# A token transform of seven matmuls in place of nine, and a new order of the work around it

## The chip, the cores and the metric

The kernel runs on one core of a Trainium2 chip. The metric is the device time of one execution in microseconds. Five engines work side by side: TensorE (PE, with its weight loads as PEld), VectorE (DVE), ScalarE (ACT), GpSimd (POOL), and SyncE (SP), which issues most of the DMA transfers.

## The reference

There are two stages. The first, for 8 batches, 8 heads, 576 tokens and a head size of 64, is a linear attention with a norm; its outputs are put side by side as x of 8 x 576 x 512. The second adds a Fourier mix to x and runs a feed-forward layer with a residual:

```python
kv = np.einsum('bhsd,bhse->bhde', k, v)
out = np.einsum('bhsd,bhde->bhse', q, kv)
out = out / np.sqrt(np.mean(out * out, axis=-1, keepdims=True) + 1e-06) * g_norm
x = out.transpose(0, 2, 1, 3).reshape(B, S, H * D)
X = np.fft.fft(np.fft.fft(x, axis=1), axis=2)
u = x + np.real(X)
un = (u - mean(u)) / np.sqrt(var(u) + 1e-06)
out = u + np.maximum(un @ w_ch1, 0.0) @ w_ch2      # 512 -> 2048 -> 512
```

The FFT over axis 1 is the token transform, the FFT over axis 2 the channel transform.

## The kernel before

**Three passes for a product.** TensorE multiplies float32 numbers rounded to a shorter form (F32R). To keep the precision, an operand is split into a high part (rounded) and a low part (what the rounding left), and a product is three matmuls: high by high, high by low, low by high. The list `passes = [(0, 0), (0, 1), (1, 0)]` stands for that.

**Stages of a batch.** The functions `plan_kv`, `plan_q`, `plan_out` and `plan_y` load k, v and q and make x with its norm, in three tiles x of 96 token pairs each (a token and its mirror lie side by side in one row of 1024 columns; tile 0 has a 97th row, token 0). `plan_fold` scales a tile by the norm (DVE, L1097), folds the channels by their symmetry into `ab` (DVE, three instructions at L1109), makes sum and difference of the two halves into `xe` (POOL, L1119, two instructions), and splits that into `xh` (ACT, L1125) and `xl` (POOL, L1128). `plan_seq` is the token transform: for each of two parts (cosine, sine) and two channel halves, nine matmuls (three tiles by three passes) of 290 columns against the constants `cs`, 36 a batch (PE, L1146). Its results go through `far` (ACT) and `pt` (DVE) to `plan_chn`, the channel transform (PE, L1192), then `x` gets its mix (POOL, L1231 and L1234; DVE for the first batch), is stored, and is turned (`plan_turn`, PE, L1290) into `unTh` and `unTl`, columns of the input of the feed-forward layer.

**The feed-forward layer** works on 9 blocks of 512 tokens. For three of the sixteen slices of w1 and w2 a block is worked off as soon as it is turned (`plan_early`, L707 and L725, 72 matmuls a block); the rest of the layer follows after the batches (L1659, L1670, then L2021, L2056), from about 310 us to the end.

**The order of the work.** Everything up to there is given as operations with an engine, an estimated cost, a rank, what they come after and which buffers of which ring they hold. `Plan.run` plays them through with these costs: on each engine the ready operation of lowest rank whose buffers are free goes next, and the order so found is pinned instruction by instruction. The early feed-forward work has a high rank (`FILL`), so it fills what the batches leave on PE. Ranks are moved by the table `SHIFT`, one number for each stage, engine and rank. Rings bound how far ahead the work runs (`RINGS`: 9 tiles x, 4 tiles e2, 7 tiles for k and v, 3 pairs xh and xl). An operation marked `port`, and every POOL operation, are kept from running side by side in the plan.

**The spares.** `plan_spare` puts 92 matmuls without a use (L778) on PE: 30 at the start and 62 of the very last rank (`SPARE`), which the plan places where nothing else is ready. Their number is fixed.

**Single points.** `dft["s", part]` are the constants of the token transform: loaded into a tile of ring x (`draw`), split by ACT (L809) and POOL (L812). `x0` collects one sum for each token and batch (L1102); after the batches nine matmuls (`p0_mm`, L1485) transform it.

Of the kernel before, what the change touches and what calls it, by code (L numbers as in the profile page):

```python
# [9 lines left out]
F32 = mybir.dt.float32  # L10
F32R = mybir.dt.float32r
# [16 lines left out]
NA = 3  # L28
# [27 lines left out]
    ("", "DVE", -100): -1448,  # L56
    ("", "POOL", -40): 17.5,
    ("", "SP DMA", -40): -10141,
    ("", "HOST", 0): 1816.5,
    ("", "POOL", 10): -5.5,  # L60
    ("", "SP DMA", 10): -746.5,
    ("", "POOL", 20): 180,
    ("", "SP DMA", 20): 2640,
    ("", "POOL", 30): 416.5,
    ("", "POOL", 40): 214,
    ("", "POOL", 50): 610.5,
    ("", "POOL", 60): 997.5,
    ("", "POOL", 70): 1564.5,
    ("", "DVE", 85): 8704.5,
    ("", "PE", 85): 2564.5,  # L70
    ("", "SP DMA", 85): 250,
    ("", "HOST", 9000): 1111.5,
    ("chn", "ACT", -34): -184.5,
    ("chn", "DVE", -34): -1439,
    ("chn", "PE", -34): -83,
    ("chn", "SP DMA", -34): 402.5,
    ("chn", "DVE", 16): 595,
    ("chn", "PE", 16): -644,
    ("chn", "POOL", 16): 6,
# [12 lines left out]
    ("chn", "PE", 46): -80,
    ("chn", "POOL", 46): 1379.5,
    ("chn", "SP DMA", 46): -3012.5,
    ("chn", "ACT", 56): 1025,
    ("chn", "PE", 56): -25901.5,
    ("chn", "POOL", 56): -528.5,
    ("chn", "SP DMA", 56): -1527,
    ("chn", "ACT", 66): -31752.5,
    ("chn", "PE", 66): -52.5,  # L100
    ("chn", "POOL", 66): -3331,
    ("chn", "SP DMA", 66): 11254,
    ("chn", "DVE", 76): 25.5,
    ("chn", "PE", 76): -133,
    ("chn", "POOL", 76): -23.5,
    ("chn", "SP DMA", 76): -103.5,
    ("dft", "ACT", -37): 96.5,
    ("dft", "POOL", -37): -769.5,
    ("dft", "SP DMA", -37): -1260,
    ("dft_d", "ACT", -35): 29,  # L110
    ("dft_d", "DVE", -35): 260.5,
    ("dft_d", "POOL", -35): 759.5,
    ("dft_d", "SP DMA", -35): -1780,
    ("early", "ACT", -100): -3365,
    ("early", "DVE", -100): -6.5,
    ("early", "SP DMA", -100): -3677.5,
    ("early", "PE", 1010): 4339.5,
    ("early", "PE", 1020): 6953.5,
    ("early", "PE", 1030): -3681,
    ("early", "PE", 1040): -4341,  # L120
    ("early", "PE", 1050): 838.5,
    ("early", "PE", 1060): 298,
    ("early", "PE", 1070): -32396.5,
    ("early", "PE", 1080): -1466,
    ("fold", "ACT", -36): 250,
    ("fold", "DVE", -36): 678,
    ("fold", "ACT", 14): -1189.5,
    ("fold", "DVE", 14): -774,
    ("fold", "POOL", 14): 151.5,
    ("fold", "ACT", 24): 2956,  # L130
    ("fold", "DVE", 24): 4653,
    ("fold", "POOL", 24): 2218.5,
    ("fold", "ACT", 34): -660,
    ("fold", "DVE", 34): 389.5,
# [2114 lines left out]
```

## Time and profile before

| what | value |
|---|---|
| time, median of 3 runs | 966.81 us (966.07 to 968.41) |
| the profiled execution's own time | 966.81 us |
| its span, first to last instruction | 965.0 us |
| PE busy | 956.7 us (99%) |
| DVE, ACT, POOL busy | 683.8, 362.6, 438.3 us |
| granted TensorE clock | 1.000 over the whole span |
| DMA | 210 MB, mean 218 GB/s |

The busy time of an engine is the time in which at least one of its instructions is running; matmuls overlap, so the duration of one (390 ns for 512 columns) is longer than the distance from one to the next. "Idle before, releaser" says how long an engine had stood before an instruction, and which instruction or transfer it had waited for.

### The profile page before, as it was taken

The page shows a single profiled execution, that of the slowest core. Times are in us where ns is not written, and L with a number is a line of the kernel's source. Part 1 is how long each engine was busy: PE and PEld are TensorE (multiplying, and loading weights), DVE is VectorE, ACT ScalarE, POOL GpSimd, SP SyncE. Part 2 cuts the span into 40 slices and gives each one's busy share as a digit, 9 for nine tenths or more (in the row PEclk, how much of TensorE's full clock was granted, in tenths as well). Part 3 has the DMA queues.
Part 4 walks back from the last instruction along what each step waited for, and adds up shares of the span by engine and source line. Part 5 has one row for each costly group of instructions (what it writes and reads, how often), then busy time and mean ns, then how long its engine had stood idle before and what let it go on. Part 6 is the DMA issues. An engine that isn't in the chain of part 4 may idle for free.

```text
span 965.0 us, 15998 instructions
## 1 busy us (share of the span) xinstructions
PE 956.7 (99%) x5992; PEld 806.7 (84%) x5992; DVE 683.8 (71%) x1192; ACT 362.6 (38%) x685; POOL 438.3 (45%) x426
## 2 busy tenths in 40 slices
PE   9999999999999999999999999999999999999998
PEld 7888888988888888888888888888888888888886
DVE  4897867766868568999547967586757685674554
ACT  2655647575544323343313421342225222521110
POOL 2646767975854215666635043825472428210000
PEclk9999999999999999999999999999999999999999
DMA  9999979572475799987588496428642675213412
GB/s 239 211 258 273 253 217 277 130 229 88 158 289 192 283 325 309 367 305 275 220 307 329 162 362 246 187 87 292 240 165 93 231 275 209 88 66 126 189 68 87
DMA packets 112193, 210.00 MB, mean 218 GB/s; under 512 B 45150, under 2 KB 66226, under 8 KB 103156
## 3 DMA queue, kind: packets, MB, share of 16 engines
q1 hardware_dynamic: 109076, 199.54, 62.6%
q0 software_dynamic: 1920, 6.29, 1.8%
q10 hardware_dynamic: 1120, 3.15, 1.0%
q8 instruction: 47, 0.77, 0.3%
q14 instruction: 30, 0.25, 0.1%
HBM read 141.02 MB, written 67.93 MB: 217 GB/s over the span
## 4 chain that ended last, share of the span: by engine, by line
PE 97%; DVE 1%; DMA 1%; issue 0%; ACT 0%; POOL 0%; DVEq 0%; POOLq 0%; ACTq 0%
PE acc L2056 23%; PE ps_h L2021 20%; PE ps_h L1659 10%; PE acc L1670 10%; PE ps_h L707 8%; PE acc L725 8%; PE ps_f L1146 4%; PE ps_o L982 3%; PE ps_k L886 3%; PE ps_s L778 2%; PE ps_f L1192 2%; PE ps_q L955 2%; PE ps_t L1290 2%; DMA vm<-in_v_dram 1%; PE ps_w L666 1%
## 5 line engine op out<-in xcount | busy, mean ns | idle before, releaser
L2056 PE MATMUL acc<-w2c,hh 128*128 128x512 f32 x640 | 197.7, 390 | 0.0
L720 DVE SCALAR_TENSOR_TENSOR hl<-ps_h,hh 128x512 fp32r<-128x512 f32 x144 | 98.7, 688 | 109.2 <-ACT hh L717 102.7
L717 ACT ACTIVATE hh<-ps_h 128x512 fp32r<-128x512 f32 x144 | 85.8, 597 | 232.2 <-PE ps_h L2021 88.4
L2056 PEld LDWEIGHTS acc<-w2c,hh 128*128 128x128 f32 x640 | 119.7, 188 | 25.4
L2066 DVE TENSOR_TENSOR us<-acc,us 128x512 f32<-128x512 f32 (+1 forms) x161 | 106.9, 681 | 43.0 <-PE acc L2056 42.6
L2056 PE MATMUL acc<-w2c,hl 128*128 128x512 f32 x320 | 124.5, 389 | 0.0
L2021 PE MATMUL ps_h<-t,w1c 128*128 128x512 f32 x480 | 115.3, 389 | 0.0
L2021 PEld LDWEIGHTS ps_h<-t,w1c 128*128 128x128 f32 x480 | 90.1, 188 | 18.7
L2021 PE MATMUL ps_h<-b,w1c 128*128 128x512 f32 x360 | 91.2, 389 | 0.0
L1692 POOL TENSOR_TENSOR us<-us,low 128x512 f32<-128x512 f32 x30 | 45.5, 1521 | 99.8 <-ACT low L1689 93.8
L2021 PEld LDWEIGHTS ps_h<-b,w1c 128*128 128x128 f32 x360 | 67.6, 188 | 14.0
L2056 PEld LDWEIGHTS acc<-w2c,hl 128*128 128x128 f32 x320 | 60.1, 188 | 12.4
L725 PE MATMUL acc<-w,hh 128*128 128x512 f32 x216 | 67.9, 398 | 0.0
L707 PE MATMUL ps_h<-unTh,w 128*128 128x512 f32 x216 | 67.4, 393 | 0.0
L1670 PE MATMUL acc<-w,hh 128*128 128x512 f32 x216 | 64.6, 390 | 0.0
L1032 POOL TENSOR_TENSOR x<-x,gb 96x512 f32<-96x512 f32 (+1 forms) x36 | 46.4, 1305 | 30.2 <-ACT x L999 29.9
L1659 PE MATMUL ps_h<-unTh,w 128*128 128x512 f32 x192 | 59.9, 393 | 0.0
L1887 POOL TENSOR_TENSOR z<-z,low 128x512 f32<-128x512 f32 x24 | 31.0, 1296 | 58.1 <-DMA low<-unT_scr 56.7
L2038 DVE TENSOR_TENSOR ps_h<-ps_h,s 128x512 f32<-128x512 f32 x60 | 39.8, 693 | 13.8 <-PE ps_h L2021 13.2
L1670 PEld LDWEIGHTS acc<-w,hh 128*128 128x128 f32 x216 | 40.5, 188 | 8.4
L2123 ACT COPY s<-ps_h 128x512 f32<-128x512 f32 x20 | 11.7, 587 | 92.8 <-PE ps_h L2021 92.8
L707 PEld LDWEIGHTS ps_h<-unTh,w 128*128 128x128 f32 x216 | 39.9, 188 | 7.9
(183 smaller groups left out, 1984.7 us busy)
## 6 DMA issues: line engine op xcount, KB each, us to landing
w1c<-w_scr SPq DMA_DIRECT2D x13, 1792.0 KB
raw<-in_moe_w_ch_dram SPq DMA_DIRECT2D x32, 512.0 KB
w2c<-w_scr SPq DMA_DIRECT2D x14, 1024.0 KB
unT_scr<-unTh SPq DMA_DIRECT2D x9, 1024.0 KB
unT_scr<-unTl SPq DMA_DIRECT2D x9, 1024.0 KB
part_scr<-part SPq DMA_DIRECT2D x36, 256.0 KB
w_scr<-w1q SPq DMA_DIRECT2D x5, 1792.0 KB
km<-in_k_dram SPq DMA_DIRECT2D x29, 288.0 KB
```

Source lines behind the costliest of these rows:

```text
L707: nc.tensor.matmul(ps, w[c][:, kc * P : (kc + 1) * P], unT[a][:, kc, :], start=(idx == 0), stop=(idx == 3 * KC - 1),)
L717: nc.scalar.activation(hh, ps, AF.Relu)
L720: nc.vector.scalar_tensor_tensor(hl, ps, 0.0, hh.bitcast(F32), ALU.max, ALU.subtract)
L725: nc.tensor.matmul(acc, hpair[a][:, i * P : (i + 1) * P], w[c], start=(first and n == 0), stop=(last and n == 2),)
L1032: nc.gpsimd.tensor_tensor(v_, v_, gb[:n].unsqueeze(1).to_broadcast([n, H, D]), ALU.mult)
L1659: nc.tensor.matmul(ps, w1_of(f, c, kc), unTs[j][a][:, kc, :], start=(idx == 0), stop=(idx == 3 * KC - 1),)
L1670: nc.tensor.matmul(acc, hpair[a][:, i * P : (i + 1) * P], w2_of(f, c), start=(first_ and n == 0), stop=(last_ and n == 2),)
L1692: nc.gpsimd.tensor_tensor(ut, ut, part, ALU.add)
L2021: nc.tensor.matmul(ps, w[:, A_OF[m], c, kc * P : (kc + 1) * P], b[:, a, kc * BT : (kc + 1) * BT], start=(fresh and idx == 0), stop=(done a ...
L2038: nc.vector.tensor_tensor(to, a, b, ALU.add)
L2056: nc.tensor.matmul(ps, hpair[a][:, i * P : (i + 1) * P], w2c[n][:, r, c], start=(idx == 0), stop=(idx == 5),)
L2066: nc.vector.tensor_tensor(ut[:, cols], ps[:, cols], ut[:, cols], ALU.add)
```

## The change

From the second batch on, the third tile of 96 rows is taken apart into three groups of 32 rows. Two of them are put into the rows 96 to 127 of tiles 0 and 1, which so have 128 rows and take three matmuls each. The rest, 32 rows of tile 2 and two rows that both hold token 0, is put into a stacked tile `xst` of 98 rows in which the same 32 rows stand three times (twice rounded, once as the low part) against constants `css` laid out to match, so that one matmul does all three passes: 3 + 3 + 1 = 7. The first batch keeps nine, with the constants of its third tile in two tiles of ring x (`third`). The constants of the new rows are loaded and split once more (`plan_dft_rest`), after the matmuls of the first batch have read the rows that they overwrite. The sum and difference of the moved rows are made by DVE (`moved`, two instructions each, three times a batch) and the stacked tile by three ACT copies in place of one. The transform of `x0` has seven matmuls too, with more small DVE copies ahead of it. Ring e2 has 5 tiles for 4, the ring for k and v 6 for 7; tile 0 has 98 rows for 97 in every stage. All numbers of the table SHIFT are other ones, so the order on every engine is a new one up to about 310 us; the code of the rest is the same.

```diff
@@ the table of shifts @@
 SHIFT = {
-    ("", "DVE", -100): -1448,
-    ("", "POOL", -40): 17.5,
...
+    ("", "DVE", -100): -546.5,
...
 }
 RINGS = {
-    "p8": 8, "part": 2, "unT": 2, "h": 2 * NA, "qt": 2, "fq": 4, "kvt": 2, "kv": 7, "kr": 2, "x": 9, "raw": 2, "e2": 4, "wk": 2, "xhl": 3, "pt": 1, "two": 2, "far": 1,
+    "p8": 8, "part": 2, "unT": 2, "h": 2 * NA, "qt": 2, "fq": 4, "kvt": 2, "kv": 6, "kr": 2, "xst": 1, "x": 9, "raw": 2, "e2": 5, "wk": 2, "xhl": 3, "pt": 1, "two": 2, "far": 1,
 }
@@ sizes @@
-    rows = [TR + 1, TR, TR]
+    rows = [TR + 2, TR, TR]
+    Q4 = P - TR
+    KST = TR + 2
+    assert TR == 3 * Q4
     offs = [0, TR + 2, 2 * TR + 2]
@@ tiles @@
-    cs = cst.tile([TR + 1, 2, 2, 3, NS], F32R, name="cs")
+    cs = cst.tile([P, 2, 2, 2, NS], F32R, name="cs")
+    css = cst.tile([KST, 2, NS], F32R, name="css")
     cd = cst.tile([P, 2, 2, NE], F32, name="cd")

     paired = cst.tile([P, 1], F32, name="paired")
     nc.vector.tensor_scalar(paired, ident[:, P - 1 : P], -1.0, 1.0, ALU.mult, ALU.add)
-    x0 = cst.tile([TR + 1, 3, B], F32, name="x0")
+    x0 = cst.tile([P, 3, B], F32, name="x0")
...
@@ plan_dft @@
         raw = ring("x", one, [P, 2 * DM], "draw")
...
+        third[part] = ring("x", one, [P, 2 * DM], "third", F32R)
         flat = src[part].rearrange("p t c -> p (t c)")
...
+        dft["s", part] = plan_dft_split(
+            r, raw, ld, slice(0, n), slice(0, 2 * NS),
+            *[lambda c=c: dst[:n, part, c].rearrange("p t c -> p (t c)") for c in range(2)],
+        ) + plan_dft_split(
+            r, raw, ld, slice(0, TR), slice(2 * NS, 3 * NS),
+            *[lambda c=c: third[part].t[:TR, c * NS : (c + 1) * NS] for c in range(2)], [third[part]],
         )
-        dft[key, part] = c
+
+    def plan_dft_split(r, raw, ld, rows_, cols, hi, lo, bufs=()):
...
+        b = op(
+            "ACT", 100 + size, r,
+            lambda: nc.scalar.activation(hi(), raw.t[rows_, cols], AF.Copy), ld, [raw, *bufs],
+        )
+        if lo is None:
+            return [b]
+        return [op(
+            "POOL", 100 + 2.25 * size, r,
+            lambda: nc.gpsimd.tensor_tensor(lo(), raw.t[rows_, cols], hi().bitcast(F32), ALU.subtract),
+            [b], [raw, *bufs],
+        )]
+
+    def plan_dft_rest(part, used):
+        r = rank(1, SEQ) - 6
+        raw = ring("x", one, [P, 2 * DM], "drest")
+        s = dft_s[part]
+        own = slice(2 * NS, 3 * NS)
+        low_rows = slice(Q4, 2 * Q4)
+
+        def free():
+            return raw.t[TR:, : 2 * NS].rearrange("p (t c) -> p t c", t=2)
+
+        ld = [
+            dma(kb, r, lambda fn=fn: nc.sync.dma_start(*fn()), [], [raw])
+            for kb, fn in (
+                (80, lambda: (free(), s[: 2 * Q4, 2].rearrange("(t p) c -> p t c", t=2))),
+                *[(40, lambda g=g: (raw.t[g * Q4 : (g + 1) * Q4, own], s[2 * Q4 : TR, 2])) for g in range(3)],
+                (4, lambda: (raw.t[TR:KST, own], s[TR, 0].partition_broadcast(2))),
+            )
+        ]
+        done = plan_dft_split(
+            r, raw, ld[:1] + used, slice(TR, P), slice(0, 2 * NS),
+            *[lambda c=c: cs[TR:, part, c].rearrange("p t c -> p (t c)") for c in range(2)],
+        )
+        h = plan_dft_split(r, raw, ld[1:], slice(0, KST), own, lambda: css[:, part], None)
+        done.append(op(
+            "POOL", 760, r,
+            lambda: nc.gpsimd.tensor_tensor(
+                css[low_rows, part], raw.t[low_rows, own], css[low_rows, part].bitcast(F32),
+                ALU.subtract,
+            ), h, [raw],
+        ))
+        dft["rest", part] = done + h
@@ plan_fold, plan_split, plan_folds @@
...
+        f = op("DVE", 860, r, fold, ms, [x, ab] + keep, port=True)
+        return f, op("DVE", 150, r, zero, ms + [i_x0], [x])
...
+        xhl = [ring("xhl", one, [P, 2, 2, DH], "xhl", F32R) for _ in range(2)]
+        st = ring("xst", one, [KST, 2, DH], "xst", F32R)
+        zs, fs = [], []
+        for t in (2, 0, 1):
+            f, z = plan_fold(b, t, xs[t], ys[t], yp, gs[t], abs_[t], [xes[t]])
+            fs.append(f)
+            zs.append(z)
+
+        def even(eng, t, lo, hi, ab, at, s):
+            o, a = halves(xes[t], at + hi - lo, at), halves(ab, hi, lo)
+            eng.tensor_tensor(o[:, s], a[:, 0], a[:, 1], ALU.subtract if s else ALU.add)
+
+        def own(t, lo, f):
+            return [op(
+                "POOL", 830, r, lambda s=s: even(nc.gpsimd, t, lo, TR, abs_[t], lo, s),
+                [f], [abs_[t], xes[t]],
+            ) for s in range(2)]
+
+        def moved(t, of, lo, hi, f):
+            return op(
+                "DVE", 660, r,
+                lambda: [even(nc.vector, t, lo, hi, abs_[of], TR, s) for s in range(2)],
+                [f], [abs_[of], xes[t]], port=True,
             )

-        return xhl, op("POOL", 1340, r, low, [h], [xe, xhl]), z
...
+        e2 = own(2, 2 * Q4, fs[0])
+        e0 = [moved(0, 2, 0, Q4, fs[0])]
+        e1 = [moved(1, 2, Q4, 2 * Q4, fs[0])]
+        e0 += own(0, 0, fs[1])
+        e2.append(moved(2, 0, TR, KST, fs[1]))
+        e1 += own(1, 0, fs[2])
+        lows = []
+        for t, e in ((0, e0), (1, e1)):
+            h = op(
+                "ACT", 640, r,
+                lambda t=t: nc.scalar.activation(xhl[t].t[:, 0], halves(xes[t]), AF.Copy),
+                e, [xes[t], xhl[t]],
+            )
+            lows.append(op(
+                "POOL", 1340, r,
+                lambda t=t: nc.gpsimd.tensor_tensor(
+                    xhl[t].t[:, 1], halves(xes[t]), xhl[t].t[:, 0].bitcast(F32), ALU.subtract
+                ),
+                [h], [xes[t], xhl[t]],
+            ))
+        hs = [op(
+            "ACT", 640, r,
+            lambda lo=lo, hi=hi, at=at: nc.scalar.activation(
+                st.t[at : at + hi - lo], halves(xes[2], hi, lo), AF.Copy
+            ),
+            e2, [xes[2], st],
+        ) for lo, hi, at in ((2 * Q4, KST, 2 * Q4), (2 * Q4, TR, 0), (2 * Q4, TR, Q4))]
+        some = slice(2 * Q4, TR + 1)
+        lows.append(op(
+            "POOL", 1340, r,
+            lambda: nc.gpsimd.tensor_tensor(
+                st.t[some], halves(xes[2], TR + 1, 2 * Q4), st.t[some].bitcast(F32), ALU.subtract
+            ),
+            hs[:1], [xes[2], st],
+        ))
+        return xhl + [st], lows + hs[1:], zs
@@ plan_seq @@
...
-            a = op("PE", 1250, r, mm, dones + [dft["s", part]], [ps, pt] + xs)
+                at = slice(ch * P, (ch + 1) * P)
+                ns = [P, P] if b else [TR + 1, TR]
+                todo = [
+                    (xs[t].t[: ns[t], a, part, at], cs[: ns[t], part, c, t])
+                    for t in range(2) for a, c in passes
+                ]
+                todo += [(xs[2].t[:, part, at], css[:, part])] if b else [
+                    (xs[2].t[:TR, a, part, at], third[part].t[:TR, c * NS : (c + 1) * NS])
+                    for a, c in passes
+                ]
+                for idx, (x_, c_) in enumerate(todo):
+                    nc.tensor.matmul(
+                        ps.t[:, :NS], x_, c_, start=(idx == 0), stop=(idx == len(todo) - 1)
+                    )
+
+            made, own = (dft["rest", part], []) if b else (dft["s", part], [third[part]])
+            a = op("PE", 970 if b else 1250, r, mm, dones + made, [ps, pt] + xs + own)
             a.dense = True
             pss.append(ps)
             mms.append(a)
+        if b == 0:
+            plan_dft_rest(part, mms[:])
         far = ring("far", one, [P, NS], "far")
@@ after the batches @@
-    x0h = cst.tile([TR + 1, 3, B], F32R, name="x0h")
-    x0l = cst.tile([TR + 1, 3, B], F32R, name="x0l")
+    x0t = cst.tile([KST, B], F32, name="x0t")
+    x0s = cst.tile([KST, B], F32R, name="x0s")
+    x0h = cst.tile([P, 2, B], F32R, name="x0h")
+    x0l = cst.tile([P, 2, B], F32R, name="x0l")
     p0t, p0u, p0r = e2_buf("p0t"), e2_buf("p0u"), e2_buf("p0r")
     ps0, ps1 = bank_buf("ps_o"), bank_buf("ps_t")
...
     def p0_in():
-        nc.vector.tensor_copy(x0h, x0)
-        nc.vector.tensor_tensor(x0l, x0, x0h.bitcast(F32), ALU.subtract)
+        nc.vector.tensor_copy(x0t[TR:KST], x0[TR:KST, 0])
+        for to in range(3):
+            nc.vector.tensor_copy(x0t[to * Q4 : (to + 1) * Q4], x0[2 * Q4 : TR, 2])
+        for t in range(2):
+            nc.vector.tensor_copy(x0[TR:, t], x0[t * Q4 : (t + 1) * Q4, 2])
+        nc.vector.tensor_copy(x0h, x0[:, :2])
+        nc.vector.tensor_tensor(x0l, x0[:, :2], x0h.bitcast(F32), ALU.subtract)
+        nc.vector.tensor_copy(x0s, x0t)
+        some = slice(2 * Q4, TR + 1)
+        nc.vector.tensor_tensor(x0s[some], x0t[some], x0s[some].bitcast(F32), ALU.subtract)

     def p0_mm():
...
+        todo = [((x0h, x0l)[a][:, t], cs[:, 0, c, t]) for t in range(2) for a, c in passes]
+        todo.append((x0s, css[:, 0]))
...
-    a = op("DVE", 300, r, p0_in, zeros)
-    a = op("PE", 1200, r, p0_mm, [a], [ps0])
+    a = op("DVE", 800, r, p0_in, zeros)
+    a = op("PE", 970, r, p0_mm, [a], [ps0])
```

## Rows read from the trace of the kernel before

**Rows 1.** The page: span, busy time, chain of waits by engine and line.
```profile
span 965.0 us, 15998 instructions
PE 956.7 (99%) x5992; PEld 806.7 (84%) x5992; DVE 683.8 (71%) x1192; ACT 362.6 (38%) x685; POOL 438.3 (45%) x426
...
PE 97%; DVE 1%; DMA 1%; issue 0%; ACT 0%; POOL 0%; DVEq 0%; POOLq 0%; ACTq 0%
```

**Rows 2.** Busy time by stretches (PE, PEld, DVE, ACT, POOL, clock, DMA share, GB/s).
```profile
0.00:75.00 75.00, 70.69 (x930) 60.89 (x931) 53.49 (x118) 36.21 (x76) 33.97 (x54) 1.00 1.05 235
75.00:300.00 225.00, 224.60 (x2113) 199.30 (x2113) 167.65 (x339) 127.87 (x279) 157.69 (x173) 1.00 0.70 208
300.00:900.00 600.00, 600.00 (x2682) 495.93 (x2682) 430.03 (x687) 189.64 (x315) 246.63 (x201) 1.00 0.64 233
900.00:965.00 65.00, 61.46 (x272) 50.55 (x270) 32.66 (x49) 8.92 (x15) 0.00 (x0) 1.00 0.24 93
```

**Rows 3.** All waits of PE: who, for whom, total us, times, longest.
```profile
PE ps_s L778 <- DVE still L773: 2.0, 1, 2.0
PE ps_k L886 <- DMA vm<-in_v_dram: 1.0, 1, 1.0
PE ps_k L886 <- issue: 1.0, 1, 1.0
PE ps_o L982 <- DVE ss L1019: 0.3, 1, 0.3
PE ps_q L955 <- DVE ss L1019: 0.3, 1, 0.3
```

**Rows 4.** Timeline of PE: first and last of batch 2's 36 transforms, and what follows.
```profile
88.46 0.52 PE L1146 MATMUL ps_f<-cs,xh 97*128 97x290 f32 x2
...
93.25 0.29 PE L1146 MATMUL ps_f<-cs,xl 96*128 96x290 f32 x1
...
93.38 0.63 PE L707 MATMUL ps_h<-unTh,w 128*128 128x512 f32 x2
```

**Rows 5.** The chain of waits: last piece, 72 matmuls of 128 rows, 512 columns.
```profile
945.14 16.33 PE acc L2056 x72
```

**Rows 6.** Timeline of PE: the nine of x0 and the next instruction.
```profile
309.42 0.49 PE L1485 MATMUL ps_o<-cs,x0h 97*8 97x290 f32 x2
...
310.68 0.39 PE L666 MATMUL ps_w<-wp,mean_t 128*128 128x128 f32 x2
```

**Rows 7.** Timeline of PE at the start: last spares, a wait, the first early feed-forward.
```profile
70.30 2.33 PE L778 MATMUL ps_s<-still 128*128 128x512 f32 x9
...
74.00 0.92 PE L886 MATMUL ps_k<-vm,km 96*64 96x64 f32 x24 [1.03 <-DMA vm<-in_v_dram]
...
78.98 0.72 PE L707 MATMUL ps_h<-unTh,w 128*128 128x512 f32 x2
```

**Rows 8.** Busy time while batches 1 to 8 run (columns as in rows 2).
```profile
24.00:312.00 288.00, 285.24 (x2892) 252.41 (x2891) 221.91 (x459) 164.84 (x361) 188.00 (x217) 1.00 0.77 213
```

**Rows 9.** Timeline of DVE: three folds (three instructions each).
```profile
106.03 2.87 DVE L1109 TENSOR_TENSOR ab<-x 97x256 f32<-97x256 f32 x3
...
111.46 0.82 DVE L1109 TENSOR_TENSOR ab<-x 96x256 f32<-96x256 f32 x3
...
115.94 1.93 DVE L1109 TENSOR_TENSOR ab<-x 96x256 f32<-96x256 f32 x3
```

**Rows 10.** Timeline of POOL in the same stretch.
```profile
106.20 1.35 POOL L1234 TENSOR_TENSOR x<-x,pm 96x510 f32<-96x510 f32 x1
107.51 1.36 POOL L1231 TENSOR_TENSOR x<-x,pm 96x514 f32<-96x514 f32 x1
```

**Rows 11.** The lines that split: count, min/median/max ns, first and last start.
```profile
L1125 ACT ACTIVATE xh<-xe x23: 606/630/655, 42.5 to 279.1; 96x512 fp32r<-96x512 f32 x15, 97x512 fp32r<-97x512 f32 x8
...
L809 ACT ACTIVATE cs<-draw x2: 931/932/933, 45.3 to 50.4; 97x870 fp32r<-97x870 f32 x2
...
L812 POOL TENSOR_TENSOR cs<-draw,cs x2: 2029/2038/2046, 46.3 to 51.4; 97x870 fp32r<-97x870 f32 x2
```

**Rows 12.** Timeline of POOL: the last low part ahead of batch 2's transform.
```profile
83.34 1.77 POOL L1128 TENSOR_TENSOR xl<-xe,xh 96x512 fp32r<-96x512 f32 x1
```

**Rows 13.** The DMA view of the first 120 us.
```profile
DMA packets 38017, 29.50 MB, mean 246 GB/s; under 512 B 24911, under 2 KB 35710, under 8 KB 37696
```

More of the change, by code (lines that the diff above doesn't have):

```diff
@@ L105 @@
[L105 to L134, printed above, removed]
@@ new lines @@
+    ("chn", "POOL", 76): 4494,
+    ("chn", "SP DMA", 76): 1036.5,
+    ("dft", "SP DMA", -37): -3761.5,
+    ("dft_d", "DVE", -35): 42,
+    ("dft_d", "POOL", -35): 149,
+    ("dft_d", "SP DMA", -35): -7066,
+    ("dft_rest", "POOL", 9): 69,
+    ("dft_rest", "SP DMA", 9): -1173.5,
+    ("dft_split", "ACT", -37): -842.5,
+    ("dft_split", "POOL", -37): 8412.5,
+    ("dft_split", "ACT", 9): -318,
+    ("early", "ACT", -100): 33.5,
+    ("early", "DVE", -100): 439.5,
+    ("early", "SP DMA", -100): 252,
@@ new lines @@
+    ("fold", "DVE", 74): 459,
+    ("folds", "ACT", 14): 6759,
+    ("folds", "DVE", 14): 1528.5,
+    ("folds", "POOL", 14): 617.5,
+    ("folds", "ACT", 24): -17.5,
+    ("folds", "DVE", 24): 10050.5,
+    ("folds", "POOL", 24): -14.5,
+    ("folds", "POOL", 34): 3446.5,
+    ("folds", "ACT", 44): 75.5,
+    ("folds", "DVE", 44): -0.5,
+    ("folds", "POOL", 44): -1471,
+    ("folds", "ACT", 54): 1716,
+    ("folds", "DVE", 54): 48795.5,
+    ("folds", "POOL", 54): 502,
+    ("folds", "ACT", 64): -7226.5,
@@ new lines @@
+    ("folds", "DVE", 64): -4042,
+    ("folds", "POOL", 64): 19,
+    ("folds", "ACT", 74): 221.5,
+    ("folds", "DVE", 74): 147.5,
+    ("folds", "POOL", 74): -179,
+    ("kv", "ACT", -40): 270.5,
+    ("kv", "DVE", -40): 297.5,
+    ("kv", "PE", -40): 595,
+    ("kv", "SP DMA", -40): -35010,
+    ("kv", "PE", 10): -1845,
+    ("kv", "SP DMA", 10): -10567,
+    ("kv", "ACT", 20): 99.5,
+    ("kv", "PE", 20): -383,
+    ("kv", "SP DMA", 20): -2303.5,
+    ("kv", "ACT", 30): 1617.5,
+    ("kv", "PE", 30): -61.5,
@@ new lines @@
+    ("w", "SP DMA", 1004): -1469,
+    ("w", "ACT", 1005): -591.5,
+    ("w", "DVE", 1005): -2792.5,
+    ("w", "PE", 1005): 570.5,
+    ("w", "POOL", 1005): -2239.5,
+    ("w", "SP DMA", 1005): -604,
+    ("y", "ACT", -37): 294.5,
+    ("y", "DVE", -37): -3531,
+    ("y", "POOL", -37): 45,
+    ("y", "ACT", 13): 1293.5,
+    ("y", "POOL", 13): -7.5,
+    ("y", "ACT", 23): 7295.5,
+    ("y", "DVE", 23): 9,
+    ("y", "POOL", 23): -1767,
+    ("y", "ACT", 33): -154,
+    ("y", "DVE", 33): 3264,
@@ new lines @@
+    third = {}
+    def plan_dft_split(r, raw, ld, rows_, cols, hi, lo, bufs=()):
+        size = cols.stop - cols.start
+        b = op(
[9 more added lines that the diff above has]
+        )]
```

584 lines of the change are left out of this document (277 added, 307 removed).

## The prediction

> **What bounds the kernel now.** Read the page first [rows 1]: PE is busy for 956.7 of 965.0 us, and the chain that ended last is PE for 97%, with no issue time to speak of. Since overlapping durations can hide small gaps, the second view is the table by stretches [rows 2]. It shows two kinds of time. From 75 us to 900 us PE is full (0.4 us missing in 225 us, none in the next 600). Ahead of 75 us it lacks 4.3 us and, more to the point, it spends time on spares: the last of them runs at 70.30 us and the first early feed-forward matmul at 78.98 us [rows 7]. So the start waits for data, and everything behind it is a queue of work on PE. Third, PE's own waits [rows 3]: five, 4.6 us together, the last of any size being the 1.0 us for v at 74.00 us [rows 7]. The rest of the 8.3 us without work is the last output's way out [rows 2]. The clock is 1.00 in every stretch [rows 2], the higher level, 2.4 GHz. In such a kernel a matmul taken away behind 75 us shortens the time by its distance to the next one, as long as the other engines go on feeding PE.
>
> **The change, part by part.**
>
> *Matmuls removed.* Batch 2's 36 transforms start at 88.46 us, and the next matmul starts at 93.38 us [rows 4]: 4.92 us, 0.1367 us each. Seven for nine take away 8 of 36, so 8 x 0.1367 = 1.093 us a batch and 7.65 us for seven batches. The transform of x0 takes 310.68 - 309.42 = 1.26 us for nine [rows 6]; two less are 0.28 us. Together 7.93 us, all of it behind 75 us.
>
> *The seven that stay are taller:* 128 or 98 rows for 96 or 97. The trace has no 290-column matmul of 128 rows. From one side, 72 matmuls of 128 rows and 512 columns take 16.33 us [rows 5], 0.227 us each or 0.443 ns a column; 290 columns at that rate are 0.128 us, less than the 0.1367 us of 97 and 96 rows. From the other, if time went with rows, the six would take 0.1367 x 128/96 = 0.182 us, seven 1.23 us, and the gain would be gone. The tall row is the nearer one, being the same engine at the same number of rows, so I take 0.1367 us as it is and count nothing for height.
>
> *Work added for DVE.* Three `moved` steps a batch, two instructions each on 256 columns, 42 instructions in all. The nearest row is the fold: three instructions, two of them of 254 or 256 elements, took 0.82 us at 111.46 us [rows 9], so some 0.33 us each with the tiny one left out, and 42 x 0.33 = 14 us. The same three took 2.87 us at 106.03 us and 1.93 us at 115.94 us [rows 9], the first while POOL ran two additions of 1.35 us one after the other [rows 10]. So a fold can lose 1.1 to 2.05 us to POOL, and if each of 21 steps lost 1.1 us, it would be 14 + 23 = 37 us. DVE was busy for 221.9 of 288 us while the batches run [rows 8], 77%. With 14 to 37 us more in 280 us it comes to 84 to 92%. It stays below PE, so I take nothing for it on the path; what hides it is the early feed-forward work, which PE can do while a batch is being folded. If that cover is gone, a batch waits for as much as the steps take (third rival).
>
> The Trainium skill's page "SBUF — State Buffer", section "SBUF: two separate sides", says that DVE with two inputs in SBUF and GpSimd take turns on one pair of ports, and that the one that comes second stands for the whole of the other's instruction. The trace agrees (2.87 us against 0.82 us) [rows 9, 10]. By it each `moved` step may stand behind one POOL instruction, which speaks against this change.
>
> *Work added for ACT and POOL.* Two more copies of 0.63 us a batch on ACT [rows 11], 8.8 us on an engine busy for 164.8 of 288 us [rows 8]. POOL has as many sums and low parts as before. Once, the constants are split for the new rows: by the 0.93 us and 2.04 us of 870 columns [rows 11], 580 + 290 columns cost as much again, two times, 1.9 us on ACT and 4.1 us on POOL, between the first batch's transforms and those of the second at 88 us. Both engines are idle for half of the first 75 us [rows 2]; I count nothing. DVE's small copies for x0 come behind the batches, with the feed-forward layer queued on PE: nothing.
>
> *Transfers added.* Ten, of 64 + 96 + 2 rows by 1160 bytes for each part, 376 KB together, on SP's queue in a time in which the DMA engines are full: 29.5 MB in the first 120 us, 246 GB/s [rows 13]. That is 1.5 us of their time. What stands behind them in the queue are k, v and q of later batches, and PE has stood for v once, for 1.0 us [rows 7]. The bounds are 0, if the loads behind are all early, and 1.5 us, if every one is late. I take half, 0.75 us, since one wait in the stretch shows that some load there has no reserve and the filling work behind it shows that most have.
>
> *Rings and order.* In the first batch `third` holds two of the nine x tiles until its transforms have read them; with three tiles of x, the two constants to be split and those of the channel transform all nine can be taken, so that the second batch gets its x later. Spares were running then, and their number is fixed, so that other work goes where spares stood: 0 on PE if the plan turns the two round, up to the 8.7 us between the last spares and the early feed-forward [rows 7] if the whole start slips. I take 0. With 5 tiles e2 the third fold of a batch must wait until one of six is free; that is on the side of DVE and POOL. The ring of 6 for k and v only bites where loads are late, as priced above. The new table of shifts changes which wait comes where; PE's waits that are not at the very start sum to 2.6 us [rows 3], so the most that a better order gives back is 2.6 us, and hidden gaps beyond that some tenths.
>
> **The sum.** The profiled execution took 966.81 us, 1.81 us more than its span, and it is itself the median of the runs. 966.81 - 7.93 + 0.75 = 959.6 us.
>
> **The rivals.**
>
> *Part of it is eaten.* The start slips, or the stacked tile is late for some batches, and PE gets waits that it didn't have. For it: the last low part ahead of batch 2's transform ends at 85.11 us [rows 12] and the transform starts at 88.46 us [rows 4], a reserve of 3.35 us, against which stand up to 2 us more on DVE and 1.3 us on ACT. Against it: PE had other work there. With 2 to 7 us of new waits: 962 to 967 us.
>
> *The folding is the bound, and the time is longer.* One mechanism: in each batch from the second on, DVE's three moved steps, at a POOL instruction's wait each (2 us + 3 x 1.1 us [rows 9]), and the two ACT copies stand between the fold and the stacked matmul, and the early feed-forward work of the block before has been used up. Up to 5.3 + 1.3 = 6.6 us a batch, less the 3.35 us of reserve, is 3.3 us; seven times that is 23 us, so 982 us at the worst. It decides from 7.93 / 7 = 1.13 us of PE wait a batch on. For it: DVE is the second busiest engine in this stage, and folds do lose time to POOL [rows 9, 10]. Against it: 0.4 us of waits in 225 us [rows 2] with folds that lost 2 us among them. With half of it, 970 to 978 us. The rule on SBUF that is quoted from the Trainium skill above speaks for this one.
>
> *A tall matmul takes longer.* The change then doesn't do what it says: seven as long as nine, 966 to 968 us. For it there is no row; against it, rows 5.
>
> *More is gained than the matmuls.* The new order also removes the 2.6 us of waits and some hidden gaps: 954 to 957 us.
>
> **How the numbers follow.** The forecast, with 957 to 962 us as its own range: 0.60. Part eaten: 0.17. Folding as the bound: 0.09. Tall matmuls: 0.04. More gained: 0.10. The predicted time is 959.6 us. From 956 to 966.5 us the range holds the forecast, nearly all of the second case and a part of the last, and leaves out about 0.19: the folding as the bound, most of the larger gain and the end of the others. A change under 0.3%, 2.9 us, can't be told from none; that is 963.9 to 969.7 us. Faster are the forecast, the larger gain and about a third of the second case: 0.75. Within are the rest of that one, the tall matmuls and the mildest end of the third case: 0.17. Slower: 0.08.
>
> **What would show it.** The table of L1146 with 36 + 7 x 28 = 232 matmuls, and 28 of them in 3.83 us from the first to the next one's start; 0.137 us each says that height costs nothing. PE's waits between 75 us and 300 us still under 1 us together; the first early feed-forward matmul again near 79 us; DVE at 84 to 92% while the batches run; the stretches behind the batches unchanged, only some 7 us earlier. It is wrong if PE waits for `xst`, `xl` or `cs` for more than a us a batch, if the spares end later than 72 us by several us, or if the distance of the tall matmuls is above 0.15 us.

## The result, and the profile after

The changed kernel takes 973.37 us (median of 8 runs, 969.95 to 974.29), the kernel before 967.35 us (8 runs, 964.66 to 968.95). The ratio is 1.0059, with an interval from 1.0042 to 1.0075: it is slower by 6 us (0.6%), where 7 us less had been forecast. The profiled execution of the changed kernel took 974.29 us. It was the slowest of the eight, with one of the lowest mean granted clocks (0.989; the eight lie between 0.989 and 0.996, the fastest at 0.996), so what follows takes one execution apart that lost more than most. Of the ten executions of e8_order one took 1927 us at a clock of 1.000, and is left out below.

The page of the changed kernel: span, busy time, the clock in 40 slices, the chain by engine.

```profile
span 972.5 us, 15968 instructions
...
PE 958.9 (99%) x5934; PEld 807.4 (83%) x5934; DVE 709.3 (73%) x1242; ACT 374.6 (39%) x705; POOL 445.4 (46%) x432
...
PEclk9989997999999999999999999999999999999999
...
PE 91%; DVE 4%; DMA 2%; POOL 1%; issue 1%; ACT 1%; SPq 0%; DVEq 0%; POOLq 0%
```

PE has 58 instructions less than in [rows 1] and is busy for 2.2 us more. Two things are new: the row PEclk has an 8 in its third and a 7 in its seventh slice (24.3 us each, so about 49 to 73 us and 146 to 170 us), and DVE has 4% of the chain, up from 1%. The stretches of [rows 2] and [rows 8], and three finer ones (columns as there):

```profile
0.00:75.00 75.00, 70.07 (x875) 60.24 (x875) 54.52 (x112) 34.99 (x76) 30.93 (x52) 0.95 0.97 219
75.00:300.00 225.00, 220.25 (x2072) 193.86 (x2070) 185.44 (x382) 138.76 (x294) 161.66 (x174) 0.97 0.70 203
300.00:900.00 600.00, 600.00 (x2692) 496.78 (x2692) 432.08 (x693) 190.78 (x319) 252.84 (x206) 1.00 0.64 233
...
24.00:312.00 288.00, 280.27 (x2790) 246.54 (x2788) 240.85 (x494) 171.47 (x368) 194.40 (x220) 0.96 0.75 207
...
48.00:75.00 27.00, 24.68 (x289) 21.80 (x289) 23.04 (x48) 13.23 (x32) 11.98 (x17) 0.87 0.86 196
...
140.00:170.00 30.00, 27.07 (x277) 23.76 (x276) 22.12 (x42) 17.53 (x37) 18.25 (x22) 0.77 0.66 208
...
154.00:167.00 13.00, 13.00 (x144) 12.28 (x142) 8.04 (x14) 7.23 (x13) 8.03 (x11) 0.50 0.49 160
```

Behind 300 us nothing has changed. From 154 to 167 us PE counts as fully busy and does 144 matmuls at a granted clock of 0.50, the lower level of 1.2 GHz; the kernel before had 1.00 throughout. "Busy" does not show this loss; the clock column does. All of the clock records put half clock at 51.04 to 57.87 us and 153.44 to 167.10 us, 20.5 us together. PE's waits, which answer to [rows 3]:

```profile
PE ps_o L1049 <- DVE unTl L1453: 2.7, 1, 2.7
PE ps_q L1022 <- DVE ss L1086: 2.0, 2, 1.2
PE ps_s L800 <- DVE still L795: 2.0, 1, 2.0
PE ps_k L953 <- DMA vm<-in_v_dram: 0.9, 3, 0.5
...
```

The 2.0 us for `still` at the very start were there before. New are one stop of 2.7 us and two of 0.8 and 1.2 us; four more, of 0.2 to 0.7 us, come to 2.0 us. Without the one for `still` PE's waits come to 7.6 us, against 2.6 us before. Here is the long one on PE's timeline (start, duration, what, [idle before it <- releaser]): the first output of batch 5 and what follows up to the next early feed-forward.

```profile
149.60 0.39 PE L746 MATMUL acc<-w,hl 128*128 128x512 f32 x1
149.92 0.38 PE L1049 MATMUL ps_o<-kvt,fq 64*98 64x64 f32 x2
152.99 5.09 PE L1049 MATMUL ps_o<-kvt,fq 64*98 64x64 f32 x62 [2.68 <-DVE unTl L1453]
158.01 4.11 PE L953 MATMUL ps_k<-vm,km 96*64 96x64 f32 x72
162.05 2.83 PE L1022 MATMUL ps_q<-ident,qt 98*128 98x98 f32 x16
164.59 1.20 PE L746 MATMUL acc<-w,hh 128*128 128x512 f32 x2
...
171.04 0.62 PE L728 MATMUL ps_h<-unTh,w 128*128 128x512 f32 x2
```

DVE's timeline in the same stretch:

```profile
145.47 1.94 DVE L1166 TENSOR_TENSOR ab<-x 96x256 f32<-96x256 f32 x3
147.44 2.51 DVE L1225 TENSOR_TENSOR xe<-ab 32x256 f32<-32x256 f32 x4
149.97 0.83 DVE L1166 TENSOR_TENSOR ab<-x 98x256 f32<-98x256 f32 x3
150.90 1.29 DVE L1225 TENSOR_TENSOR xe<-ab 2x256 f32<-2x256 f32 x2
152.20 3.17 DVE L1453 TENSOR_TENSOR unTl<-ps_t,unTh 128x384 fp32r<-128x384 f32 x8
```

And POOL's:

```profile
147.55 1.79 POOL L1225 TENSOR_TENSOR xe<-ab 32x256 f32<-32x256 f32 x2 [0.50 <-DVE ab L1166]
150.94 1.83 POOL L1225 TENSOR_TENSOR xe<-ab 96x256 f32<-96x256 f32 x2 [1.61 <-DVE ab L1166]
```

Batch 4's `moved` steps (L1225 on DVE) stand ahead of `unTl`, which DVE reads out of the PSUM banks of turned x; outputs share the one ring of 8 banks with everything else, and PE stands until the first of them is read. Nearly all of the outputs behind the stop then run at half clock.

**Where the time went.** The next table is worked out from PE's records. Each matmul counts with the distance that its shape has in undisturbed stretches (0.227 us for 512 columns, 0.134 for 290, 0.11 for 130, 0.083 for a turn, 0.047 for an output, 0.035 for k by v), and all beyond that, spares included, is lost time of its stretch. The distances are estimates, so the entries are good to some tenths; each column is one profiled execution. The last three columns are experiments of the next section.

| us | before | after | e2_no_moved | e10_one_batch | e12_all_pool |
|---|---|---|---|---|---|
| matmuls | 923.2 | 915.4 | 915.4 | 915.4 | 915.4 |
| lost, 0 to 48 us | 23.2 | 23.0 | 22.6 | 23.1 | 23.5 |
| 48 to 82 | 8.7 | 12.7 | 10.1 | 12.9 | 10.2 |
| 82 to 140 | 1.4 | 1.5 | 1.6 | 1.7 | 2.2 |
| 140 to 170 | 1.6 | 10.2 | 1.6 | 1.7 | 1.6 |
| 170 to 310 | 2.1 | 4.6 | 2.8 | 5.2 | 4.3 |
| 310 to the end | 4.7 | 5.0 | 5.2 | 5.0 | 5.0 |
| span | 965.0 | 972.5 | 959.4 | 965.1 | 962.3 |

So 7.8 us of matmuls went, as forecast, and 15.3 us of loss came: 8.6 in the stretch of the long stop, 4.0 at the start, 2.5 from 170 to 310 us.

### The profile page after: what moved, and what is told of

The parts are those of the page before. It is cut to its first block, busy times and chain, and to the rows that moved or that the text cites. A ratio compares the mean times of both kernels' runs of the same rounds, so it can differ in the third digit from the quotient of the medians.

```text
span 972.5 us, 15968 instructions
## 1 busy us (share of the span) xinstructions
PE 958.9 (99%) x5934; PEld 807.4 (83%) x5934; DVE 709.3 (73%) x1242; ACT 374.6 (39%) x705; POOL 445.4 (46%) x432
## 4 chain that ended last, share of the span: by engine, by line
PE 91%; DVE 4%; DMA 2%; POOL 1%; issue 1%; ACT 1%; SPq 0%; DVEq 0%; POOLq 0%
PE acc L2207 22%; PE ps_h L2172 20%; PE ps_h L1810 10%; PE acc L1821 10%; PE ps_h L728 7%; PE acc L746 7%; PE ps_o L1049 3%; PE ps_f L1299 3%; PE ps_k L953 2%; DMA vm<-in_v_dram 2%; PE ps_f L1343 2%; PE ps_s L800 2%; PE ps_q L1022 1%; PE ps_t L1441 1%; DVE ab L1166 1%
## 5 line engine op out<-in xcount | busy, mean ns | idle before, releaser
L1049 PEld LDWEIGHTS ps_o<-kvt,fq 64*96 64x96 f32 (+1 forms) x864 | 41.1, 169 | 7.8 <-DVE unTl L1453 2.8
L1049 PE MATMUL ps_o<-kvt,fq 64*96 64x64 f32 (+1 forms) x864 | 44.4, 256 | 3.1 <-DVE unTl L1453 2.7
```

The lines of the kernel that those rows point to most:

```text
L1049: nc.tensor.matmul(pss[s].t[:n, at : at + D], fqs[side].t[half, m, :n], kvt.t[half, m], start=True, stop=True,)
```

## Experiments

Theory A: the `moved` steps on DVE delay what PE needs next; the stops are small, but the clock falls behind them. Rivals: the new order is worse by itself, the matmuls are worth less than counted, or the clock falls for another reason. Each kernel is timed against the kernel before on the same chip.

**Spares in the stops (e1_fill).** From the changed kernel; 3 and 5 spares ahead of two turned q at 50 and 52 us, 11 ahead of batch 5's first output.

```diff
...
         def turn():
+            for _ in range({0: 3, 2: 5}.get(j, 0) if b == 2 and side == 0 else 0):
+                spare[0]()
...
         def mm(pss=pss, kvt=kvt):
+            for _ in range(11 if b == 4 and t == 0 else 0):
+                nc.tensor.matmul(pss[0].t, still, spare[1], start=True, stop=True)
```

> The changed kernel with nothing taken away, but 19 spare matmuls more, put on PE just ahead of instructions that stood waiting: 3 and 5 ahead of two of batch 3's q transposes (near 50 and 52 us, where PE stood 0.80 and 1.24 us), 11 ahead of the first output of batch 5 (near 150 us, where it stood 2.68 us). They use banks that PE already holds, so the work waited for comes no earlier. Theory A (the clock): the two drops of the granted clock, at 51.04 us for 6.83 us and at 153.44 us for 13.66 us, follow from these stops; with PE kept at work the clock stays at 1.00 throughout, and half of 20.5 us comes back: 974 - 9 = 963 to 966 us, with the same waits now hidden under spares. Theory B (the clock falls because the matmuls in that stretch are short, 64 columns and less, whatever the stop): both drops stay, 972 to 976 us.

Measured: 967.44 us (before 967.41; ratio 1.0011, 0.9993 to 1.003), just above the range of theory A, with no half clock in the profiled execution. The `moved` steps are where they were, and 75 to 300 us reads

```profile
75.00:300.00 225.00, 222.79 (x2099) 195.67 (x2098) 191.20 (x392) 139.99 (x297) 163.90 (x177) 1.00 0.74 213
```

By the ratios (1.0059 and 1.0011) matmuls of no use in place of idle time give about 5 us back. They can't replace the wait; what they keep is the clock. They don't keep it every time: seven of the ten executions took 966.7 to 968.1 us at a mean clock of 0.999 or more, three had 0.995 to 0.997 and took 969.1 to 973.7 us.

**No moved steps (e2_no_moved).** From the changed kernel, order kept. The lines that are not shown take the transform down to 96 rows, so that 64 token pairs and token 0 are left out of it.

```diff
-                lambda: [even(nc.vector, t, lo, hi, abs_[of], TR, s) for s in range(2)],
+                lambda: None,
...
```

> The changed kernel without the 42 DVE instructions of the moved steps; what they would have written is not used (the transform of batches 2 to 8 takes 96 rows for 128 and 98, so that 64 token pairs and token 0 are missing from it). The order on every engine and the number of matmuls are as in the changed kernel. Theory A (the moved steps, each standing behind POOL instructions, push DVE's later work back, and PE's wait near 150 us for the low parts of the turned tiles is that): PE's wait of 2.68 us near 150 us falls under 0.5 us, the second drop of the clock is gone, PE's waits behind 75 us sum to under 1.5 us: 963 to 967 us. Theory B (the new order puts these waits there, with or without the moved steps): the wait near 150 us stays above 2 us and the time stays at 970 to 974 us.

Measured: 963.72 us (ratio 0.9957, 0.9941 to 0.9974); the profiled span is 959.4 us. The long stop is down to

```profile
PE ps_o L1049 <- DVE unTl L1453: 0.3, 1, 0.3
```

and its profiled execution has no half clock. So the change without its `moved` steps is faster than the kernel before; the 42 instructions on DVE turn it.

**Nine matmuls again (e3_nine).** Two of the seven run twice.

```diff
+                if b:
+                    for x_, c_ in todo[:2]:
+                        nc.tensor.matmul(ps.t[:, :NS], x_, c_, start=True, stop=True)
```

> The changed kernel with two more matmuls in each group of seven from the second batch on (the first two are made twice, the first time for nothing), so nine again, in the same order and with all the rest of the change. If a matmul taken away is worth its distance of 0.1367 us, as the prediction had it, this one is 56 x 0.1367 = 7.65 us slower than the changed kernel: 980 to 983 us. If the changed kernel's time is set by DVE and POOL instead (folding as the bound), the two more fill waits and it is 0 to 3 us slower: 973 to 977 us. In theory A of the clock there may be a smaller difference if PE, being at work for longer, waits less near 150 us.

Measured: 979.53 us (ratio 1.0117, 1.01 to 1.0134), by the ratios some 5.6 us more than the changed kernel, with the stop of 2.7 us unchanged. That is less than the 7.65 us counted and just under the range of 980 to 983 us. The profiled execution differs in other losses too: near 52 us it has half clock for 3.41 us, where the changed kernel had 6.83. So most of what was counted for the matmuls is there; the rival, that the two more only fill waits, expected 0 to 3 us.

**A slower reduction in the kernel before (e5_before_wait).** One DVE reduction of batch 5 five times over, to lengthen a stop of 0.3 us.

> The kernel before, with one reduction of DVE made five times over instead of once (same input, same output; the second half of tile 2 of batch 5, near 147 us, where PE stands 0.31 us for it in the kernel before). That puts some 2.4 us on DVE and makes PE's wait there 2.5 to 2.8 us. Theory A (a stop of PE of that length is enough for the clock to fall, whatever the kernel): a stretch of 3 to 14 us at half clock right after it, and the time is the 2.4 us plus half of that stretch longer: 971 to 977 us. Theory B (the fall needs the changed kernel's stretch of short matmuls around the stop, 130 of 64 columns and less behind it, while here 30 + 8 follow and then wide ones): the clock stays at 1.00 and the time grows by 2.4 us at most: 967.5 to 970 us.

Measured: 967.85 us (ratio 1.0019, 1.0003 to 1.0034). The stop stayed at 0.31 us: PE stood for the reduction just before the repeated one. So this says nothing on the clock, only that 2.9 us more on DVE, from 147.9 to 150.7 us, made no new wait of PE there.

**Wide matmuls behind the stop (e6_behind).** From the changed kernel, 11 spares of 512 columns behind batch 5's outputs.

```diff
+                for _ in range(11 if b == 7 and pr == 0 else 0):
+                    nc.tensor.matmul(ps.t, still, spare[1], start=True, stop=True)
```

> The changed kernel with 11 wide spare matmuls put on PE behind the outputs of batch 5 that wait near 150 us, ahead of the 72 short ones of batch 8's k and v. The stop stays at 2.7 us. Theory A (the clock falls after the stop, and comes back when PE has wide work): the fall near 153 us is there, but ends earlier than 167.1 us, by 3 us or more; the 2.5 us of spares at full clock and up to half of what is won nearly cancel: 971 to 975 us. Theory B (the fall lasts a fixed time): it lasts 13.7 us as in the changed kernel and the spares come on top, 976 to 980 us.

Measured: 975.69 us (ratio 1.0092, 1.0072 to 1.0112). PE's timeline:

```profile
153.57 4.96 PE L1056 MATMUL ps_o<-kvt,fq 64*98 64x64 f32 x62 [2.68 <-DVE unTl L1460]
158.47 3.95 PE L957 MATMUL ps_k<-still 128*128 128x512 f32 x11
162.34 2.32 PE L960 MATMUL ps_k<-vm,km 96*64 96x64 f32 x72
```

The table by stretches, columns as in [rows 2]:

```profile
154.00:161.00 7.00, 7.00 (x64) 6.40 (x61) 5.52 (x11) 4.91 (x9) 3.48 (x3) 0.51 0.01 4
161.00:172.00 11.00, 11.00 (x140) 9.19 (x140) 6.11 (x12) 5.32 (x12) 5.44 (x9) 1.00 0.70 245
```

The same stop, but the clock is back to 1.00 at 161 us, after 6.83 us at half in place of 13.66, before the 72 short matmuls, which take 2.32 us for 4.11. That fits theory A, in one execution. It doesn't show that the wide matmuls end the fall: the other three executions have a mean clock of 0.990 (0.993 in this one), as low as most of the changed kernel's, and were not profiled. In time the spares bring nothing: by the ratios the kernel is 3 us slower than the changed one, between the two theories' ranges.

**The added DVE work in the kernel before (e7_before_moved).** 42 sums behind its folds, written to rows of `xe` that nothing reads.

```diff
+            for s in range(2 if b else 0):
+                a = ab.t[:32, :DM].rearrange("p (s d) -> p s d", s=2)
+                o = xe.t[96:, :DM].rearrange("p (s d) -> p s d", s=2)
+                nc.vector.tensor_tensor(o[:, s], a[:, 0], a[:, 1], ALU.add)
```

> The kernel before, with two more DVE instructions after each fold from the second batch on: sums of 32 rows and 256 columns, of the kind and number (42) that the change adds, into rows that nobody reads. Order and all else as before; the plan's costs don't know of them. Theory A (the added DVE work is enough to delay what PE waits for): PE's waits behind 75 us grow from 0.6 us to 3 us or more, perhaps with a fall of the clock: 970 to 978 us. Theory B (the old order has reserve for it, and it was the new order that placed PE's outputs right behind DVE's folds): the waits stay under 2 us and the time under 969.5 us.

Measured: 990.27 us (ratio 1.0245, 1.0223 to 1.0266), with these waits:

```profile
PE ps_t L1294 <- DVE unTl L1306: 3.4, 1, 3.4
PE ps_o L982 <- DVE ss L1019: 2.4, 1, 2.4
PE ps_f L1196 <- DVE pt L1180: 2.3, 1, 2.3
PE acc L725 <- DVE unTl L1306: 2.3, 1, 2.3
```

This is above the range of both theories. The profiled execution has half clock twice, for 10.24 us from 77.44 us, behind the stop of 3.4 us, and for 6.83 us from 224.21 us, within the stop of 2.3 us for `acc`. The other two, of 2.32 and 2.40 us, lie in this stretch, without a fall:

```profile
140.00:170.00 30.00, 25.28 (x309) 22.48 (x309) 25.26 (x49) 15.81 (x35) 19.99 (x20) 1.00 0.58 158
```

In the old order the same number of added sums on DVE costs 24 us: in the profiled execution PE's stops grow by some 13 us, and 17.07 us of half clock cost about half of that. So the delay through DVE is not peculiar to the new order. That the new order holds most of it off is likely, and not shown: here the sums stand inside the folds, and the rings differ too.

**Another order (e8_order) and the same with spares (e9_order_fill).** The changed kernel with another table SHIFT, sought so that PE waits little even where DVE and POOL block each other; then with the 19 spares of e1_fill.

> The changed kernel, nothing else in it changed than the numbers of the table SHIFT, which were chosen so that PE waits less for DVE also when DVE and POOL get in each other's way at every fold and moved step. If the loss is in where the order puts PE's work behind the moved steps (theory A), an order that reckons with them gets part of the 7.9 us back: PE's waits behind 75 us under 4 us, at most one fall of the clock, 961 to 969 us. If it is in the added DVE work whatever the order (theory B), the time stays at 970 to 975 us.

> The kernel of the run beside it with the 19 spare matmuls of the first experiment at the same instructions (3 and 5 ahead of two q transposes of batch 3, 11 ahead of the first output of batch 5). If a long stop near 150 us is left and the clock falls there (theory A), the spares keep it at 1.00: 960 to 966 us, 2 us or more under the run beside it. If no long stop is left there, or the clock falls for another reason (theory B), the spares only cost: 0 to 4 us more than the run beside it.

Measured: 973.55 us (median of nine; ratio 1.0044, 1.0022 to 1.0065) and 974.54 us (1.0062, 1.0045 to 1.008). Both miss what theory A expected. Both keep a stop of 2.7 us for `unTl`, ending at 157.03 and 154.99 us, and a fall behind it; in the second the spares ran ahead of another output. The order wasn't repaired, so these say little on the cause; an order without the stop was not found, and whether there is one stays open.

**One batch's moved steps on POOL (e10_one_batch), the same with spares at the start (e11_one_batch_fill), all on POOL (e12_all_pool).** From the changed kernel; six instructions change the engine (shown), or all 42 (without the condition). The second also has the 3 and 5 spares of e1_fill.

```diff
-                lambda: [even(nc.vector, t, lo, hi, abs_[of], TR, s) for s in range(2)],
+                lambda: [even(nc.gpsimd if b == 3 else nc.vector, t, lo, hi, abs_[of], TR, s) for s in range(2)],
```

> The changed kernel with the six moved instructions of one batch alone, batch 4, given to POOL in the place where DVE had them; everything else, and the order, as it is. In the changed kernel these six took DVE 2.51 us at 147.44 us and 1.29 us at 150.90 us, and the only long stop of PE (2.7 us, for unTl) ended right behind them. Theory A (these steps delay unTl, the stop they cause is what the clock falls behind): the stop goes down to under 0.5 us, the clock stays at 1.00 from 140 to 170 us, and the 8.6 us that this stretch lost more than before come back: 973.4 - 8 = 965.5 us, 964 to 968. Rival B (the sums are on the way to batch 4's transforms wherever they are made, and POOL makes them no faster, some 0.85 us each, so 5.1 us more in POOL's chain): a new wait of PE of 2 to 5 us for xl, xst or x between 150 and 165 us, and 971 to 976 us. Rival C (the clock falls for a reason that is not the stop): the stop goes and the half clock stays, 970 to 971 us.

> As the run before it (batch 4's six moved instructions on POOL), and with 3 and 5 spares put into the two stops of PE at 50 and 52 us, ahead of batch 3's first and third turned q. Theory A: no half clock at all; 6.83 us of half clock at 51 to 58 us less, worth about 3.4 us, on top of the other: 965.5 - 3.4 = 962 us, 960 to 965, below the kernel before by 2 to 6 us. Rival B: 968 to 973 us, with the wait for POOL's results still there.

> The changed kernel with all 42 moved instructions on POOL in place of DVE. POOL was busy for 161.7 of the 225 us from 75 to 300 us; 36 more instructions there at about 0.85 us are 31 us, so 86%, and DVE comes down from 185 to about 170 us. Theory A (DVE being late is the cause, and POOL has the room): no stop of over 1 us from 75 to 300 us, clock 1.00 there, 965 to 968 us. Rival B (whichever engine makes them, the port pair and the chain are the limit): several waits of 1 to 4 us on POOL's results, and 972 to 985 us.

Measured: 966.09 us (ratio 0.9986, 0.9975 to 0.9996), 965.16 us (0.9978, 0.9967 to 0.9989) and 966.44 us (0.9982, 0.9969 to 0.9994). By the ratios all three beat the changed kernel by 7 to 8 us and the kernel before by 1 to 2 us. The first and the third lie in the range of theory A, the second just above it. In e10_one_batch, PE's timeline at the place of the stop:

```profile
150.38 0.91 PE L1049 MATMUL ps_o<-kvt,fq 64*98 64x64 f32 x16
151.75 2.27 PE L1049 MATMUL ps_o<-kvt,fq 64*98 64x64 f32 x48 [0.46 <-POOL fq L1032]
153.94 2.32 PE L953 MATMUL ps_k<-vm,km 96*64 96x64 f32 x72
156.19 1.55 PE L1022 MATMUL ps_q<-ident,qt 98*128 98x98 f32 x16
...
162.79 0.62 PE L728 MATMUL ps_h<-unTh,w 128*128 128x512 f32 x2
```

Its DVE:

```profile
145.92 2.65 DVE L1166 TENSOR_TENSOR ab<-x 96x256 f32<-96x256 f32 x6
148.49 3.20 DVE L1453 TENSOR_TENSOR unTl<-ps_t,unTh 128x384 fp32r<-128x384 f32 x8
```

Its POOL:

```profile
146.82 4.71 POOL L1225 TENSOR_TENSOR xe<-ab 32x256 f32<-32x256 f32 x6 [0.80 <-DVE ab L1166]
```

The clock from 140 to 170 us is back:

```profile
140.00:170.00 30.00, 29.30 (x345) 24.88 (x344) 24.84 (x50) 22.48 (x47) 25.42 (x33) 1.00 0.85 255
```

`unTl` starts 3.7 us earlier, and the same matmuls, from batch 5's first output to the next early feed-forward, take 162.79 - 150.38 = 12.4 us for 171.04 - 149.92 = 21.1 us. Of these 8.7 us the wait is 2.2 (2.68 less 0.46) and half clock the rest, 6.5. Rival B, that POOL's results come late instead, doesn't appear: its waits there are 0.5 us. Rival C, a fall for another reason, doesn't either. In the second of the three the fall at 51 us is gone, but the profiled execution has one at 78 to 85 us, behind stops of 0.46 and 0.84 us, which takes part of the gain: at a mean clock of 1.000 its runs take 963.6 to 965.5 us, below that up to 968.2. The third, with all 42 on POOL at 0.73 us each (median), says that POOL had the room, with no stop above 0.7 us from 75 to 300 us:

```profile
75.00:300.00 225.00, 221.85 (x2098) 195.01 (x2097) 178.51 (x359) 140.56 (x298) 191.56 (x216) 1.00 0.72 214
```

## Why the prediction was wrong, by its own steps

*Matmuls removed* was right: 7.93 us counted, 7.8 us fewer in the table, and some 5.6 us when they are put back. *Height* was right too; batch 2's transforms, first and last rows and what follows, which answer to [rows 4]:

```profile
90.17 1.05 PE L1299 MATMUL ps_f<-cs,xhl 128*128 128x290 f32 x6
91.06 0.30 PE L1299 MATMUL ps_f<-css,xst 98*128 98x290 f32 x1
...
94.12 1.60 PE L1049 MATMUL ps_o<-kvt,fq 64*98 64x64 f32 x32
```

28 in 3.95 us are 0.141 us each, the first of them slower. From 180.74 to 181.68 us, in batch 4, seven take 0.94 us, 0.134 us each:

```profile
180.74 0.97 PE L1299 MATMUL ps_f<-cs,xhl 128*128 128x290 f32 x6
...
181.68 0.97 PE L1299 MATMUL ps_f<-cs,xhl 128*128 128x290 f32 x6
```

[rows 5] were the right neighbour.

*Work added for DVE* is the step that failed, and not in its size (the sign that was named for it, a wait for `xst`, `xl` or `cs`, did not come):

```profile
L1225 DVE TENSOR_TENSOR xe<-ab x42: 409/422/1667, 73.5 to 276.8; 32x256 f32<-32x256 f32 x28, 2x256 f32<-2x256 f32 x14
```

At 0.42 us (median) and up to 1.67 us behind POOL they come to 25.5 us, within the 14 to 37 us counted, and DVE to 240.85 of 288 us, 84%, the lower end of what was said. Wrong was "so I take nothing for it on the path", with the early feed-forward as the cover. That covers a late transform, and indeed PE never waits for `xst` or `xl`. But what stood behind the added steps on DVE was not only the fold's own results: `unTl` of another batch did too (`moved` ends and `unTl` starts at 152.2 us), and its banks hold up PE's outputs, in PE's fixed order, with nothing that could go ahead of them. The prediction names the ports, 1.1 us a step, and names no other work queued behind a step. One place in seven batches was enough, a stop of 2.68 us; an average of 84% says nothing of it.

*The clock* was not in the sum at all. "The clock is 1.00 in every stretch" was read from a kernel whose stops behind the very start are 1.0 us at most; a stop was priced at its length. Here one of 2.68 us cost 8.7 us, three quarters of it as half clock over short matmuls. The Trainium skill's page "TensorE: Matmul & The Clock Gate", section "HAM oscillation — how this bites in real kernels", describes a kernel whose PE waits some 3 to 5 us for data before each tile, and whose next tile then starts at the lower clock. The traces here show the same behind a shorter stop, of 2.68 us (0.50 from 154 to 167 us, 1.00 with the stop filled or gone), though not behind every stop of that size, as the last section has it.

*Rings and order, the start* was taken as 0, up to 8.7 us; it is 4.0 us, so a part of the rival "the start slips" came true, and one of the prediction's own signs with it: the last spares run at 76.45 us for 70.30 [rows 7]. The first early feed-forward starts at 81.45 us for 78.98 [rows 7], behind these stops and 6.83 us of half clock:

```profile
50.28 0.56 PE L1022 MATMUL ps_q<-ident,qt 98*128 98x98 f32 x4 [0.80 <-DVE ss L1086]
52.07 0.90 PE L1022 MATMUL ps_q<-ident,qt 96*128 96x96 f32 x4 [1.24 <-DVE ss L1086]
```

In e12_all_pool, with the stops there but the clock at 1.00, 1.5 us of it remain; the clock's share of the 4.0 is so about 2.5 us. The stops don't come from the `moved` steps, for e2_no_moved has them too; whether the new order, `third` or the rings make them was not tested.

*Transfers* were counted at 0.75 us; PE's waits for v are 0.9 us in all, 1.0 before, so nothing of it shows. Added up by the table, which makes this no check of its own: 966.81 - 7.9 + 8.6 (stop and clock) + 4.0 (start) + 2.5 (170 to 310 us) + 0.3 (the end) = 974.3 us, the profiled execution. The 2.5 us weren't taken apart; 1.8 of them are gone in e2_no_moved, so most seem to hang on the `moved` steps as well, on POOL too (4.3 us in e12_all_pool).

Of the rivals, the folding as the bound named the right engine, with the wrong victim and rhythm: it asked for 1.13 us of wait in every batch, and all of PE's waits grew by 5 us in seven batches. That the measured time lies in its 970 to 978 us is luck, for it had no half clock in its sum. "Part of it is eaten" reached to 967 us and held no clock.

## What to carry to other kernels

An added step on an engine that is not the bound has to be followed in that engine's own queue: list what comes behind it, of whichever batch, and ask for each who holds a buffer until it is done. A stop of TensorE can cost more than its length: look at the clock column behind each one, and fill or move a stop that a fall follows. When one step of many does the harm, moving that one to another engine (six instructions here) brings as much as moving all.

## What was not expected of the hardware

A stop of 2.68 us was followed by 13.66 us at 1.2 GHz in the changed kernel's profiled execution, with short matmuls behind it, and by 6.83 us in that of e6_behind, with 512-column ones behind it; with one execution of each it is not shown that the width made the difference. Length alone doesn't decide whether the clock falls: in e7_before_moved stops of 2.32 us at 150 us and 2.40 us at 160 us left the clock at 1.00 (its row of 140 to 170 us above), while one of 2.29 us at 225 us had a fall. The pair of 0.8 and 1.24 us at 50 us went with a fall in the changed kernel, from 51.04 us, inside the second of the two, and in e10_one_batch, not in e2_no_moved or e12_all_pool. What tells these apart stays open. In a kernel with such stops the time of a run goes with its mean clock (964.3 us at 1.000 to 967.8 at 0.996 in e10_one_batch), but that is not all of the spread: the kernel before, timed beside it, took 964.8 to 968.7 us at a clock of 1.000.
